# A transformer layer's forward and backward pass on one core: the FFN of chunk 0 placed inside the last attention chunk, and the gradient stage's inputs placed in the memory of FFN weights split into parts

## The chip, the cores and the metric

The kernel runs on one core of a Trainium2 chip. The metric is the device time of one execution in microseconds (us); the smaller the better. A core has TensorE (PE) for matrix products, VectorE (DVE) and ScalarE (ACT) for elementwise work, GpSimd (POOL), which here mostly issues DMAs, and SyncE (SP), which only issues DMAs. Every engine runs its own instructions in order, and they wait for each other by semaphores.

## The reference

One layer with sliding-window attention and an FFN, and the gradients of all its inputs for a given `grad_out`. S is 2048 tokens, D is 512, F is 1792, with 32 heads of 16; everything is bf16.

```python
def attention(x, wqkv, wo):
    q, k, v = split(x @ wqkv)                 # 32 heads of 16
    idx = pos[:, None] - 2 * arange(8)        # 8 keys, every second token back
    logits = einsum("hsd,hswd->hsw", q, k[idx]) * 16 ** -0.5     # masked where idx < 0
    o = einsum("hsw,hswd->hsd", softmax(logits), v[idx])
    return merge_heads(o) @ wo

h  = x + attention(layernorm(x), wqkv, wo)
h2 = h + gelu(layernorm(h) @ w1 + b1) @ w2 + b2
out_0 = h2
out_1 .. out_7 = gradients of (x, wqkv, wo, w1, b1, w2, b2) for grad_out
```

## The kernel before, in words

Tokens are cut into NC = 4 chunks of CH = 512 (four tiles of P = 128 partitions, so DC = 4 tiles of D and FT = 14 tiles of F). There are three stages, each with its pools of SBUF memory. A pool that is released gives its bytes to the next one on the same side, and the first writer of a new tile there then waits for the last readers and writers of the old one.

**Attention** (functions `p1_*`). For each chunk: layer norm (`p1_ln`, DVE with bn_stats), the projections to q, k, v, dots over the eight taps, softmax (`p1_sm1`, `p1_sm2`), then for the output rows `R` gathered from memory by POOL's indirect DMA, eight products `prb` on DVE (L289) reduced by `ps_band` on PE (L294), the permutation back, `wo`, and `h` with the second layer norm, whose result is stored (`ln_d`) and transposed to `ln2T` (L189, L190). `p1_tm` makes the stored forms of q, k and v through the staging tile `tmst` (stores at L242 and L246). The output of a chunk is done in two halves, `p1_o(c, 0)` and `p1_o(c, 1)`, and `p1_d(c)` is its end (the transposition to `ln2T`). The pools `early` (right side: wqkv, xt, tmst and so on) and `late` (left side) serve this stage; `wff` holds `w1` and `w2`, loaded by POOL in two DMAs during chunk 0.

**FFN, forward and backward in one pass over the chunks.** `p2_h(c)` is a generator: for each of four blocks of F (4, 4, 4 and 2 tiles) it makes `ps_h` on PE (L548), bias and square on ACT (L550, L551), and the gelu with its derivative on DVE, nine operations a block (L555 to L564), around one tanh on ACT. The results `gt` and `dt_` are kept, and `gt` is transposed by a DMA on SP into `tst` and stored to `gT_d` by POOL (`tok_store`, L529 to L533). `p2_rest(c)` loads `goT` (grad_out transposed by DMA), makes the output `ps_f2` (L582) and `h2s`, then `ps_gg` = w2T by goT (L595), multiplied with dt on DVE (L598) and stored as `ghT_d`, then `ps_gl2` with w1T (L607) and the layer norm's backward. The loop over chunks runs `p2_h(c + 1)` a block at a time between groups of `p2_rest(c)`. The transposed weights `w1T` and `w2T` are made by two transposing DMAs on SP (L509, L511), and w2T is halved by one DVE operation (L510). `woT` and `wqT` are transposed at the start of chunk 2, `wkT` and `wvT` at the start of chunk 3; all four lie in buffers that were `ln2T` of the chunks (`lnt`), so that they wait for these chunks' `ps_h` to be done. `glf` is the row buffer of dots gradients, with a memset of its end at L504.

In these two stages the order of instructions on each engine is chosen by a scheduler from the order of the text, the dependencies and estimated durations; the order of the text is only its priority.

**Gradients** (from L690). The order is written out by hand. DVE's band products of the backward (`prb`, L906, 96 of 1.2 us) lead, and `slot()` fills PE with the weight gradients of the generator `wgrads`: `ps_gw2` (L789), `ps_gw1` (L798), `ps_gwo` (L808), `ps_gwq` (L818). Their inputs come through two rotating buffers in the pool `gwp`: `r8` (three of 1 MB; gout_r, ln2_r, o_r, ln1_r in halves) and `gwm` (two of 1 MB; pieces of `gT_d`, `ghT_d`), and their results leave through `gwst` (two). `p3` holds the rest: `cf`, `sh`, `ghT`, `got`, `ln1r`, `rows` and others.

Of the kernel before, what the change touches and what calls it, by code (L numbers as in the profile page):

```python
# [36 lines left out]
def kernel(  # L37
# [232 lines left out]
    def coefs(wp, src, off, hs):  # L270
        cf = wp.tile([P, 2, 2, 8, H], BF16, name="cf", tag="cf", bufs=2)
        if hs == 512:
            V.transpose(out=cf[:].rearrange("p a b c h -> p (a b c h)"), in_=_sub(src, [[256, 4], [1, 8], [8, 32]], off))
        else:
            for hf in range(2):
                V.transpose(out=cf[:, hf].rearrange("p b c h -> p (b c h)"),
                            in_=_sub(src, [[256, 2], [1, 8], [8, 32]], off + hf * hs))
        return cf
# [42 lines left out]
    w1 = wff.tile([P, DC, F], BF16, name="w1")  # L321
    w2 = wff.tile([P, FT, D], BF16, name="w2")
# [12 lines left out]
    def p1_ln(c):  # L335
        xt = early.tile([P, TPC, D], BF16, name="xt", tag="xt", bufs=4)
        load_rows(xt, xf, c)
        if c == 0:
            for i in range(3):
                o = (1, 0, 2)[i] * D  # L340
                SY.dma_start(out=wqkv[:, :, o:o + D], in_=A_wqkv[:, o:o + D].rearrange("(a p) j -> p a j", p=P))
        ln1 = early.tile([P, TPC, D], BF16, name="ln1", tag="ln1", bufs=1)
        layernorm(early, xt, rstd1, c, ln1)
        store_rows(ln1_d, c, ln1)
        ln1T = early.tile([P, DC, CH], BF16, name="ln1T", tag="ln1T", bufs=2)
        to_fm(ln1, ln1T)
        st_[c].update(xt=xt, ln1T=ln1T)
# [120 lines left out]
    G.dma_start(out=w1[:], in_=B_w1.rearrange("(a p) f -> p a f", p=P))  # L468
    G.dma_start(out=w2[:], in_=B_w2.rearrange("(a p) d -> p a d", p=P))
    p1_tm(0)  # L470
    for c in range(NC):
        if c + 2 < NC:
            p1_ln(c + 2)
        if c + 1 < NC:
            p1_dots(c + 1)
        if c > 0:
            p1_d(c - 1)
        if c + 2 < NC:
            p1_qk(c + 2)
        if c + 1 < NC:  # L480
            p1_sm1(c + 1)
        p1_o(c, 0)
        if c + 1 < NC:
            p1_v(c + 1)
            p1_sm2(c + 1)
        p1_o(c, 1)
        if c + 1 < NC:
            p1_tm(c + 1)
        if c == 1:
            V.tensor_scalar(out=w2[:], in0=w2[:], scalar1=0.5, scalar2=None, op0=ALU.mult)  # L490
    p1_d(NC - 1)

    pb = TT("pb1")
    T.transpose(pb[:, 0:FT], b1b[:], ident[0:FT, 0:FT])
    V.tensor_copy(out=b1c[:], in_=pb[:, 0:FT])
# [5 lines left out]
    late.release()  # L501
    glp = LP("glp", "right")
    glf = glp.tile([P, 2, SP], BF16, name="glf")
    V.memset(glf[:, :, S:SP], 0.0)  # L504
    ff = LP("ff", "right")
    wfb = LP("wfb")
    w1T = wfb.tile([P, FT, D], BF16, name="w1T")
    w2T = wfb.tile([P, DC, F], BF16, name="w2T")
    SY.dma_start_transpose(out=w2T[:], in_=B_w2)  # L509
    V.tensor_scalar(out=w2T[:], in0=w2T[:], scalar1=0.5, scalar2=None, op0=ALU.mult)  # L510
    SY.dma_start_transpose(out=w1T[:], in_=B_w1)  # L511
# [3 lines left out]
    def load_wT(name, src):  # L515
# [3 lines left out]
    FFT = dict(goT=([P, DC, CH], 1), tst=([P, 16, P], 3), gout=([P, TPC, D], 1), ln2r=([P, TPC, D], 1), dt_=([P, 4, 512], 5),  # L519
               h2s=([P, D], 2), gyr=([P, D], 2), junk=([P, D], 1), u=([P, D], 2), gt=([P, 4, 512], 5),  # L520
               xb=([P, 4, PAD + CH], 2), xa=([P, 2, 4, 512], 2))

    def ft(tag, name=None):
        shp, nb = FFT[tag]
        return ff.tile(shp, BF16, name=name or tag, tag=tag, bufs=nb)
# [9 lines left out]
    def p2_h(c):  # L535
        d = ps2[c]
        d["g"], d["d"] = [], []
        for (f0, f1) in FB:
# [4 lines left out]
            for fp in range(f0, f1, 2):  # L543
                ps = X("ps_h")
                for i in range(2):
                    f = fp + i
                    for dc in range(DC):
                        T.matmul(ps[:, i, :], lhsT=w1[:, dc, f * P:(f + 1) * P], rhs=ln2T[c][:, dc, :],  # L548
                                 start=(dc == 0), stop=(dc == DC - 1))
                    A.activation(out=xb[:, f - f0, :], in_=ps[:, i, :], func=ACT.Identity, bias=b1c[:, f:f + 1])  # L550
                    A.activation(out=x2[:, f - f0, :], in_=ps[:, i, :], func=ACT.Square, bias=b1c[:, f:f + 1])  # L551
            gt = ft("gt")
            dt_ = ft("dt_")
# [16 lines left out]
    def p2_rest(c):  # L570
# [8 lines left out]
        for j in range(TPC):  # L579
            ps = Y("ps_f2")  # L580
            for f in range(FT):
                T.matmul(ps[:], lhsT=gts[f // 4][:, f % 4, j * P:(j + 1) * P], rhs=w2[:, f, :], start=(f == 0), stop=False)  # L582
            T.matmul(ps[:], lhsT=ones_row[:], rhs=b2row[:], start=False, stop=False)
            T.matmul(ps[:], lhsT=ident[:], rhs=h_all[c][:, j, :], start=False, stop=True)
            h2s = ff.tile([P, D], BF16, name="h2s", tag="h2s", bufs=2)
            A.copy(out=h2s[:], in_=ps[:])
            G.dma_start(out=h2f[c * CH + j * P:c * CH + (j + 1) * P, :], in_=h2s[:])
            yield
        for bi, (f0, f1) in enumerate(FB):
            for fp in range(f0, f1, 2):  # L590
                ps = X("ps_gg")
                for i in range(2):
                    f = fp + i
                    for dc in range(DC):
                        T.matmul(ps[:, i, :], lhsT=w2T[:, dc, f * P:(f + 1) * P], rhs=goT[:, dc, :],  # L595
                                 start=(dc == 0), stop=(dc == DC - 1))
# [7 lines left out]
        for j in range(TPC):  # L604
            ps = Y("ps_gl2")
            for f in range(FT):
                T.matmul(ps[:], lhsT=dts[f // 4][:, f % 4, j * P:(j + 1) * P], rhs=w1T[:, f, :],  # L607
                         start=(f == 0), stop=(f == FT - 1))
            t = c * TPC + j
            ln_bwd(ff, ps[:], ln2[:, j, :], rstd2[:, t:t + 1], gout[:, j, :], gh[:, j, :])  # L610
            yield
# [25 lines left out]
    def p3_pre():  # L637
# [7 lines left out]
        to_tm_store(ff, got, 0, go_d, 0, False, stage=lambda: ft("tst", "tmst0")[:, 0:8, :].rearrange("p (a b) f -> p a (b f)", a=2))  # L645
# [19 lines left out]
    run(p2_h(0))  # L665
    for c in range(NC):
# [8 lines left out]
        for k in (4, 4, 3):  # L675
            run(hn, 1)
            run(r_, k)
        run(hn, 1)
        if c == NC - 1:
            pre = p3_pre()  # L680
            for _ in range(TPC):
# [8 lines left out]
    ff.release()  # L690
    wfb.release()
    wff.release()
# [4 lines left out]
    gwp = LP("gwp", "right")  # L697
    wqkvT = [wT[n] for n in ("wqT", "wkT", "wvT")]
    P3T = dict(rows=([P, 10, 512], 3), vw=([P, 4, PAD + CH], 1), ghT=([P, DC, CH], 1), got=([P, 4, CH], 1), gqkvT=([P, 12, CH], 1),
               tmst=([P, 2, 512], 2), prod=([P, W, 512], 3), ln1r=([P, TPC, D], 1), pp=([P, 2, 512], 1), sh=([P, 2, 512], 2),  # L700
               cf=([P, 2, 2, 8, H], 2), gqs=([P, 2, 512], 2), gks=([P, 2, 512], 2), gyr=([P, D], 2))

    def pt3(tag, name=None):
        shp, nb = P3T[tag]
# [12 lines left out]
    def wg_out(pss, dst, r0, c0, width=D, sca=1.0):  # L717
        st = gwp.tile([P, 2, D], BF16, name="gwst", tag="gwst", bufs=2)
# [5 lines left out]
    def load_half(name, src, i):  # L724
        r = gwp.tile([P, HN, D], BF16, name=name, tag="r8", bufs=3)
        SY.dma_start(out=r[:], in_=src[i * HN * P:(i + 1) * HN * P, :].rearrange("(t p) d -> p t d", p=P))
        return r

    def load_perm(name, src, i):
        r = gwp.tile([P, HN, D], BF16, name=name, tag="r8", bufs=3)  # L730
# [7 lines left out]
    def load_t(src, q):  # L738
        t_ = gwp.tile([P, 2, NT, P], BF16, name="gwm", tag="gwm", bufs=2)
        SY.dma_start(out=t_[:].rearrange("p a t f -> p (a t f)"),  # L740
                     in_=src[:, 2 * q:2 * q + 2].rearrange("p a c n -> p (a c n)"))
        return t_

    def load_g3(sel, i):
        if sel == 2:
            t_ = pt3("rows", "gqh")[:, 0:HN, :]
        else:
            t_ = gwp.tile([P, HN, D], BF16, name="gqh", tag="gwm", bufs=2)
# [22 lines left out]
    gout_r = [load_half("gout_r", gof, 0)]  # L771
    tiles = [load_t(gT_d, 0)]
    gout_r.append(load_half("gout_r", gof, 1))
    tiles.append(load_t(gT_d, 1))

    def wgrads():
        ln2_r = [load_half("ln2_r", ln2_d, 0)]
        o_r = []
        for q in range(7):
            if q == 6:  # L780
# [4 lines left out]
                st = gwp.tile([P, 2, D], BF16, name="gwst", tag="gwst", bufs=2)  # L785
# [4 lines left out]
                mid=(lambda: ln2_r.append(load_half("ln2_r", ln2_d, 1))) if q == 6 else None)  # L790
# [3 lines left out]
        o_r.append(load_half("o_r", o_d, 0))  # L794
        for q in range(7):
            g_ = tiles[7 + q]
            for d2 in range(2):
# [3 lines left out]
                    mid=(lambda: o_r.append(load_half("o_r", o_d, 1))) if q == 6 and d2 == 1 else None)  # L801
# [4 lines left out]
        ln1_r = [load_perm("ln1_r", ln1_d, 0)]  # L806
        for k2 in range(2):
# [3 lines left out]
                mid=(lambda: ln1_r.append(load_perm("ln1_r", ln1_d, 1))) if k2 == 1 else None)  # L811
# [115 lines left out]
    def p3_go(c, at=(1, 2, 3, 4)):  # L927
# [13 lines left out]
        def t():  # L941
            to_tm_store(p3, got, 0, go_d, c, False, 2)
# [45 lines left out]
    for c in range(NC + 2):  # L988
# [20 lines left out]
        if c > 0:  # L1009
# [4 lines left out]
            cfv = coefs(p3, st3[c - 1]["sh"][:, 0, 0:1], 0, 512)  # L1014
# [23 lines left out]
        if c < NC:  # L1038
            cfq = coefs(p3, glf[:, 0, 0:1], c * CH, SP)
# [16 lines left out]
        if c > 0:  # L1056
            cfk = coefs(p3, shk[:, 0, 0:1], 0, 512)
# [26 lines left out]
    gwp.release()  # L1084
# [36 lines left out]
```

## Time and profile before

| | us |
|---|---|
| median of 14 runs | 764.92 |
| lowest and highest of them | 756.45, 771.39 |
| the profiled execution, its time | 754.44 |
| the profiled execution, span of the trace | 752.7 |
| PE busy | 625.1 (83%) |
| DVE busy | 531.9 (71%) |
| ACT busy | 369.5 (49%) |
| mean granted TensorE clock | 0.966 |

All times of single instructions in this document come from the one profiled execution and count from its span's start. A row of a timeline gives start, duration, engine with line, operation, tiles, the number of instructions joined in the row, and in brackets the idle time of the engine before it with what released it. A row of a windows table gives the window's limits and length, busy time and number of instructions of each engine, then the granted TensorE clock (1.00 is full), the share of DMA engines that were busy, and GB/s moved. PEclk on the page is the granted clock in 40 slices, in tenths.

### The profile page before, as it was taken

The numbers are of one execution on the slowest core, as the hardware profiler recorded it, in microseconds if no ns is written. First come the engines' busy times: TensorE is split into PE (matmuls) and PEld (weight loads), VectorE is DVE, ScalarE is ACT, GpSimd is POOL, SyncE is SP. The second block draws the span as 40 slices with busy tenths as digits, with TensorE's granted clock in tenths as the row PEclk, the third lists the DMA queues.
The fourth block names the chain that finished last, engine by engine and source line by source line (L and its number), as shares of the span: only waits on it lengthen the run. The fifth ranks groups of instructions, "written<-read, shape, count | busy, mean of one in ns | idle before, by whom it ended". The sixth has DMA issues, their size and how long they took to land. (4 is left out here: it accounts for less than half of the span.)

```text
span 752.7 us, 10189 instructions
## 1 busy us (share of the span) xinstructions
PE 625.1 (83%) x3887; PEld 290.4 (39%) x3948; DVE 531.9 (71%) x774; ACT 369.5 (49%) x561; POOL 153.9 (20%) x195
## 2 busy tenths in 40 slices
PE   3787788576777888888899879979967899898997
PEld 1343343222223333333333433434335566543443
DVE  7779869664986777686695598987857688569400
ACT  2476676547553464455351253583347336554411
POOL 4122434330021021012011114140221014112100
PEclk9999999876899999999999999999989999999999
DMA  8572637758955494395488899976695567898351
GB/s 291 202 269 80 232 108 260 248 133 157 223 107 140 91 265 110 99 261 152 112 169 216 214 326 363 413 267 239 208 403 188 209 220 272 323 290 236 143 160 43
DMA packets 145967, 158.88 MB, mean 211 GB/s; under 512 B 94349, under 2 KB 130238, under 8 KB 139262
## 3 DMA queue, kind: packets, MB, share of 16 engines
q1 hardware_dynamic: 122142, 72.73, 36.7%
q0 software_dynamic: 15888, 79.72, 30.2%
q10 hardware_dynamic: 7888, 5.77, 2.4%
q8 instruction: 31, 0.51, 0.3%
q14 instruction: 18, 0.15, 0.1%
HBM read 87.63 MB, written 48.03 MB: 180 GB/s over the span
## 5 line engine op out<-in xcount | busy, mean ns | idle before, releaser
L906 DVE TENSOR_TENSOR prb<-R,cf 128x2048 bf16<-128x2048 bf16 x96 | 111.3, 1217 | 20.7 <-PE ps_band L914 15.9
L548 PE MATMUL ps_h<-ln2T,w 128*128 128x512 bf16 x222 | 63.0, 410 | 22.8 <-ACT xa L551 18.6
L798 PE MATMUL ps_gw<-gwm,ln_r 128*128 128x256 bf16 x448 | 55.6, 276 | 15.8 <-ACT gwst L721 9.4
L595 PE MATMUL ps_gg<-goT,w2T 128*128 128x512 bf16 x218 | 53.8, 378 | 11.4 <-DVE gb1p L598 8.6
L550 ACT ACTIVATE xb<-ps_h,b1c 128x512 bf16<-128x512 f32 x56 | 38.2, 686 | 43.7 <-PE ps_h L548 42.6
L582 PE MATMUL ps_f<-w,gt 128*128 128x512 bf16 x217 | 53.6, 385 | 2.6 <-DVE gt L559 2.3
L789 PE MATMUL ps_gw<-gout_r,gwm 128*128 128x512 bf16 x215 | 51.6, 380 | 4.2 <-ACT gwst L721 1.8
L355 PE MATMUL ps_qkv<-ln1T,wqkv 128*128 128x512 bf16 x186 | 48.7, 398 | 7.0 <-ACT kt L357 2.0
L798 PEld LDWEIGHTS <-ln_r 128*128 128x128 bf16 x448 | 42.9, 98 | 29.5 <-issue 16.3
L211 ACT ACTIVATE gyr<-ps_gl,rstd 128x512 bf16<-128x512 f32 x32 | 21.9, 686 | 64.0 <-PE ps_gl L970 32.5
L620 DVE TENSOR_TENSOR pr<-got,vw 128x4096 bf16<-128x4096 bf16 x16 | 36.5, 2291 | 14.3 <-ACT c L213 7.0
L548 PEld LDWEIGHTS <-w 128*128 128x128 bf16 x224 | 22.9, 103 | 57.6 <-issue 39.5
L533 POOL DMA_DIRECT2D gT_d<-tst x16 | 12.3, 772 | 156.4 <-DMA tst<-gt 151.7
L818 PE MATMUL ps_gwq<-gqh,ln_r 128*128 128x512 bf16 x188 | 42.4, 379 | 1.4 <-ACT gwst L721 1.1
L289 DVE TENSOR_TENSOR prb<-R,cf 128x2048 bf16<-128x2048 bf16 x32 | 37.3, 1211 | 7.6 <-PE ps_band L294 4.4
L557 ACT ACTIVATE xa<-xa 128x2048 bf16<-128x2048 bf16 (+1 forms) x16 | 27.2, 1698 | 30.1 <-DVE xa L556 30.1
L259 DVE TENSOR_TENSOR pr<-qt,kt 128x4096 bf16<-128x4096 bf16 x16 | 36.0, 2284 | 5.5 <-ACT qt L357 3.4
L551 ACT ACTIVATE xa<-ps_h,b1c 128x512 bf16<-128x512 f32 x56 | 38.1, 685 | 1.6 <-DVE dt__2676 L564 0.4
L916 ACT ACTIVATE gks<-ps_band 128x512 bf16<-128x512 f32 x32 | 19.0, 598 | 39.4 <-PE ps_band L914 34.4
L914 PE MATMUL ps_band<-prb,S 128*32 128x512 bf16 x384 | 30.6, 388 | 8.6 <-ACT got L617 4.4
L595 PEld LDWEIGHTS <-w2T 128*128 128x128 bf16 x224 | 21.6, 97 | 41.4 <-issue 18.5
L240 ACT COPY tmst<-ptm 128x1024 bf16<-128x1024 bf16 x32 | 31.5, 1017 | 6.9 <-PE ptm L237 4.6
(242 smaller groups left out, 1191.6 us busy)
## 6 DMA issues: line engine op xcount, KB each, us to landing
gwm<-gT_d SPq DMA_DIRECT2D x7, 1024.0 KB
gwm<-ghT_d SPq DMA_DIRECT2D x7, 1024.0 KB
gT_d<-tst POOLq DMA_DIRECT2D x12, 512.0 KB, 3.5
ghT_d<-tst POOLq DMA_DIRECT2D x12, 512.0 KB, 5.4
ln_d<-ln POOLq DMA_DIRECT2D x8, 512.0 KB, 4.7
out_dram<-gwst ACTq DMA_DIRECT2D x15, 256.0 KB
w<-in_B_w_dram POOLq DMA_DIRECT2D x2, 1792.0 KB, 10.3
vw<-vf_d SPq DMA_DIRECT2D x4, 528.0 KB
```

The source lines that it names most:

```text
L289: V.tensor_tensor(out=pr[:, hf].rearrange("p j (d h) -> p j d h", h=H), in0=R[:, o:o + 4, :].rearrange("p j (d h) -> p j d h", h=H), in1=c ...
L355: T.matmul(ps[:, gg, :], lhsT=wqkv[:, dc, sel * D + g * P:sel * D + (g + 1) * P], rhs=st_[c]["ln1T"][:, dc, :], start=(dc == 0), stop=(dc ...
L548: T.matmul(ps[:, i, :], lhsT=w1[:, dc, f * P:(f + 1) * P], rhs=ln2T[c][:, dc, :], start=(dc == 0), stop=(dc == DC - 1))
L550: A.activation(out=xb[:, f - f0, :], in_=ps[:, i, :], func=ACT.Identity, bias=b1c[:, f:f + 1])
L551: A.activation(out=x2[:, f - f0, :], in_=ps[:, i, :], func=ACT.Square, bias=b1c[:, f:f + 1])
L582: T.matmul(ps[:], lhsT=gts[f // 4][:, f % 4, j * P:(j + 1) * P], rhs=w2[:, f, :], start=(f == 0), stop=False)
L595: T.matmul(ps[:, i, :], lhsT=w2T[:, dc, f * P:(f + 1) * P], rhs=goT[:, dc, :], start=(dc == 0), stop=(dc == DC - 1))
L620: V.tensor_tensor(out=pr, in0=got[:, g, :].unsqueeze(1).to_broadcast([P, W, 512]), in1=_sub(vw[:, g, PAD:PAD + 512], [[-DIL, W], [1, 512]] ...
L789: pss = yield from mm_pair("ps_gw2", lambda ps, o, i, t, k: T.matmul(ps[:], lhsT=g_[:, o, i * HN + t, :], rhs=gout_r[i][:, t, :], **k), MM ...
L798: pss = yield from mm_pair("ps_gw1", lambda ps, o, i, t, k: T.matmul(ps[:, 0:256].rearrange("p (a f) -> p a f", a=2), lhsT=ln2_r[i][:, t, ...
L818: pss = yield from mm_pair("ps_gwq", lambda ps, o, i, t, k: T.matmul(ps[:], lhsT=ln1_r[i][:, t, (2 * d2 + o) * P:(2 * d2 + o + 1) * P], rh ...
L906: V.tensor_tensor(out=pr[:, 4 * hf:4 * hf + 4].rearrange("p j (d h) -> p j d h", h=H), in0=R[:, o:o + 4, :].rearrange("p j (d h) -> p j d ...
```

## The change

Four things are done.

1. `w1` and `w2` are held as three parts (tiles 0 to 7, 8 to 11, 12 and 13 of F), `w2T` likewise and `w1T` as four (0 to 7, 8 and 9, 10 and 11, 12 and 13). The two loads become six, the two transposing DMAs seven, and the two DVE operations that halve w2 and w2T become three each. The functions `wcol` and `wrow` pick the part. The numbers of matmuls and of their columns are the same.
2. The last attention round ends after `p1_o(3, 0)`. Then `early` is released, `glp` and a first FFN pool `ffA` (xa, xb, tst, and two of the five slots of gt and dt) take its memory; block 0 of chunk 0's `p2_h` is put ahead of `p1_o(3, 1)` and block 1 ahead of `p1_d(3)`. Then `late` is released, the second FFN pool `ffB` (the rest) and `wfb` follow, with the seven transposes. The chunk 3 input tile `xt` lies in `late` in place of `early`. The transposition of the bias b1 into `b1c` moves to the end of round 0. The memset of `glf` is written behind the generator's end.
3. The FFN pools are no longer all released ahead of the gradient stage: `wff` and `wfb` stay to the end, and tiles of the gradient stage take the parts' places by name: the `r8` halves 0 and 1 in `w10` and `w20`, `gwm` in `w2T0` and `w1T0`, `gwst` in `w1T10` and `w1T12`, `cf` in `w2T12` and `w1T8`, `sh` in `w112` and `w212`, and `ghT`, `got`, `ln1r` in `w18`, `w28`, `w2T8`. The pool `gwp` is gone. The numbers of buffers are as before.
4. The two loads of gout_r and the first `gwm` are issued on ACT's DMA queue during the last FFN chunk (before: on SP at the start of the gradient stage).

```diff
-    w1 = wff.tile([P, DC, F], BF16, name="w1")
-    w2 = wff.tile([P, FT, D], BF16, name="w2")
+    W3 = [(0, 8), (8, 12), (12, 14)]
+    W4 = [(0, 8), (8, 10), (10, 12), (12, 14)]
+    def wparts(pl, name, parts, byrow):
+        return [(a, b, pl.tile([P, b - a, D] if byrow else [P, DC, (b - a) * P], BF16, name=f"{name}{a}", tag=f"{name}{a}", bufs=1))
+                for (a, b) in parts]
+    w1 = wparts(wff, "w1", W3, False)
+    w2 = wparts(wff, "w2", W3, True)
...
-        xt = early.tile([P, TPC, D], BF16, name="xt", tag="xt", bufs=4)
+        xt = (early if c < NC - 1 else late).tile([P, TPC, D], BF16, name="xt", tag="xt", bufs=NC - 1 if c < NC - 1 else 1)
...
-    G.dma_start(out=w1[:], in_=B_w1.rearrange("(a p) f -> p a f", p=P))
-    G.dma_start(out=w2[:], in_=B_w2.rearrange("(a p) d -> p a d", p=P))
+    for a_, b_, t_ in w1:
+        G.dma_start(out=t_[:], in_=B_w1[:, a_ * P:b_ * P].rearrange("(a p) f -> p a f", p=P))
+    for a_, b_, t_ in w2:
+        G.dma_start(out=t_[:], in_=B_w2[a_ * P:b_ * P, :].rearrange("(a p) d -> p a d", p=P))
...
         p1_o(c, 0)
+        if c == NC - 1:
+            return
...
-    p1_d(NC - 1)
-    pb = TT("pb1")
-    T.transpose(pb[:, 0:FT], b1b[:], ident[0:FT, 0:FT])
-    V.tensor_copy(out=b1c[:], in_=pb[:, 0:FT])
+        if c == 0:
+            pb = TT("pb1")
+            T.transpose(pb[:, 0:FT], b1b[:], ident[0:FT, 0:FT])
+            V.tensor_copy(out=b1c[:], in_=pb[:, 0:FT])
...
     early.release()
-    late.release()
     glp = LP("glp", "right")
     glf = glp.tile([P, 2, SP], BF16, name="glf")
-    V.memset(glf[:, :, S:SP], 0.0)
-    ff = LP("ff", "right")
-    wfb = LP("wfb")
-    w1T = wfb.tile([P, FT, D], BF16, name="w1T")
-    w2T = wfb.tile([P, DC, F], BF16, name="w2T")
-    SY.dma_start_transpose(out=w2T[:], in_=B_w2)
-    V.tensor_scalar(out=w2T[:], in0=w2T[:], scalar1=0.5, scalar2=None, op0=ALU.mult)
-    SY.dma_start_transpose(out=w1T[:], in_=B_w1)
+    ffA = LP("ffA", "right")
...
+    def block_tiles():
+        k = nblk[0] % NS
+        nblk[0] += 1
+        pl = ffA if k < SA else ffp["B"]
+        return [pl.tile([P, 4, 512], BF16, name=f"{n}{k}", tag=f"{n}{k}", bufs=1) for n in ("gt", "dt")]
...
-    run(p2_h(0))
+    hn = p2_h(0)
+    run(hn, 1)
+    p1_o(NC - 1, 1)
+    run(hn, 1)
+    p1_d(NC - 1)
+    late.release()
+    ffp["B"] = LP("ffB", "right")
+    wfb = LP("wfb")
+    w2T = wparts(wfb, "w2T", W3, False)
+    w1T = wparts(wfb, "w1T", W4, True)
+    for a_, b_, t_ in w2T:
+        SY.dma_start_transpose(out=t_[:], in_=B_w2[a_ * P:b_ * P, :])
+    for _, _, t_ in w2T:
+        V.tensor_scalar(out=t_[:], in0=t_[:], scalar1=0.5, scalar2=None, op0=ALU.mult)
+    for a_, b_, t_ in w1T:
+        SY.dma_start_transpose(out=t_[:], in_=B_w1[:, a_ * P:b_ * P])
+    run(hn)
+    V.memset(glf[:, :, S:SP], 0.0)
...
+    def mtile(name, shp):
+        k = ngm[0] % 2
+        ngm[0] += 1
+        return wfb.tile(shp, BF16, name=name, tag=("w2T0", "w1T0")[k], bufs=1)
...
         for k in (4, 4, 3):
             run(hn, 1)
             run(r_, k)
+            if c == NC - 1 and k == 4 and not gout_r:
+                gout_r += [load_half("gout_r", gof, i, i, A) for i in range(2)]
         run(hn, 1)
         if c == NC - 1:
+            tiles = [load_t(gT_d, 0, A)]
...
-    gwp = LP("gwp", "right")
...
+    HOME = dict(ghT=([P, DC, CH], (wff, "w18")), got=([P, 4, CH], (wff, "w28")), ln1r=([P, TPC, D], (wfb, "w2T8")),
+                sh=([P, 2, 512], (wff, "w112"), (wff, "w212")), cf=([P, 2, 2, 8, H], (wfb, "w2T12"), (wfb, "w1T8")),
+                gwst=([P, 2, D], (wfb, "w1T10"), (wfb, "w1T12")))
...
-    gout_r = [load_half("gout_r", gof, 0)]
-    tiles = [load_t(gT_d, 0)]
-    gout_r.append(load_half("gout_r", gof, 1))
     tiles.append(load_t(gT_d, 1))
```

## The prediction, made before the changed kernel ran

> **What bounds the kernel now.** I read the page's engine rows first, then sums over windows, then the timelines of DVE, PE and SP where the windows show no engine full.
>
> ```profile
> PE 625.1 (83%) x3887; PEld 290.4 (39%) x3948; DVE 531.9 (71%) x774; ACT 369.5 (49%) x561; POOL 153.9 (20%) x195
> PEclk9999999876899999999999999999989999999999
> 140.00:173.00 33.00, 18.84 (x111) 8.05 (x111) 19.29 (x38) 12.93 (x20) 9.30 (x14) 0.75 0.73 202
> 173.00:200.00 27.00, 19.08 (x58) 7.16 (x60) 19.53 (x21) 19.81 (x29) 0.76 (x1) 0.74 0.92 193
> 200.00:229.00 29.00, 21.67 (x87) 8.23 (x87) 21.51 (x27) 17.55 (x25) 4.82 (x7) 0.94 0.62 127
> 161.30:184.80 23.50, 15.25 (x63) 6.61 (x65) 10.19 (x21) 15.31 (x22) 3.94 (x6) 0.75 0.99 191
> 710.00:752.00 42.00, 38.30 (x174) 17.02 (x176) 3.89 (x12) 8.18 (x16) 1.62 (x3) 1.00 0.30 98
> ```
>
> PE leads, but it is not one bound. The 89 us from the last chunk's bands to the first ps_gg have PE at 60 of 89 and DVE at 60, with the granted clock (third figure from the end of a row) at 0.75 in the first 60: the boundary of attention and FFN, where engines wait for each other. The last 42 us are PE at 38.3 with DVE nearly idle: the weight gradients that are left over. So the gradient stage is bound by PE, and idle PE removed anywhere moves the end.
>
> The boundary, by what ended each wait (DVE, then PE, then SP):
>
> ```profile
> 148.26 2.36 DVE L289 TENSOR_TENSOR prb<-R,cf 128x2048 bf16<-128x2048 bf16 x2 [3.09 <-DMA R<-v_d,rowi]
> 166.57 0.07 DVE L504 MEMSET glf<- 128x16 uint32 x1
> 172.92 0.17 DVE L495 CAST b1c<-pb 128x14 f32<-128x14 bf16 x1 [2.07 <-PE pb L494]
> 179.83 0.69 DVE L555 TENSOR_SCALAR xa<-xa 128x2048 bf16<-128x2048 bf16 x1 [6.74 <-ACT xa L551]
> 216.00 0.69 DVE L555 TENSOR_SCALAR xa<-xa 128x2048 bf16<-128x2048 bf16 x1 [1.64 <-ACT xa L551]
> 149.54 0.62 PE L294 MATMUL ps_band<-prb,S 128*32 128x512 bf16 x4 [6.13 <-DVE prb L289]
> 228.72 1.53 PE L595 MATMUL ps_gg<-goT,w2T 128*128 128x512 bf16 x5 [0.20 <-ACT xa L551]
> 141.65 0.36 SPq L242 DMA_DIRECT2D q_d<-tmst  x1
> 161.34 8.41 SPq L509 DMA_TRANSPOSE w2T<-in_B_w_dram  x1
> 169.89 10.28 SPq L511 DMA_TRANSPOSE w1T<-in_B_w_dram  x1
> 186.47 1.92 SPq L532 DMA_TRANSPOSE tst<-gt  x1
> 188.84 2.09 SPq L574 DMA_TRANSPOSE goT<-in_grad_out_dram  x1
> 201.37 3.10 SPq L517 DMA_TRANSPOSE woT<-in_A_wo_dram  x1
> 451.86 0.82 PE L789 MATMUL ps_gw<-gout_r,gwm 128*128 128x512 bf16 x3 [1.54 <-DMA gwm<-gT_d]
> ```
>
> Between the last band and the first gelu, DVE waits 3.69 (before 162.49), 1.37, 1.14, 2.07 and 6.74: 15 us with nothing to do, while chunk 0's gelu could run, had it been released. Its first gelu operation is at 179.83, its last ends at 214.36. SP's row is free from 142 to 161.
>
> **The change part by part.**
>
> *Begin the FFN early.* In the changed order 40 of the 56 ps_h matmuls of chunk 0 come ahead of the end of chunk 3's wo, some inside the 6.13 gap; blocks 0 and 1 of the gelu stand between and behind the eight prb. But the scheduler also puts the memset of glf directly ahead of the first prb. It takes memory of the staging tile tmst, and so waits for the q_d stores. The one of 141.65 is slow: the DMA row of 139 to 153 moves bytes until about 152.3, its completion comes at 152.58. Before, the memset ran at 166.57 and waited for nothing. All bands are queued behind it on DVE, and PE's ps_band behind those: they start at 152.58, not 148.26, **+4.3**.
>
> From there DVE is full: eight prb and the row op 9.3, ln 1.3, two gelu blocks 16.2 (four TENSOR_SCALAR at 0.62 and five TENSOR_TENSOR at 1.1 make 8.1), four bn pairs at 0.78 = 3.1, first ops 0.6: 30.5, so block 1 ends at 183.1. xa has two buffers, so the last ps_h needs that, one activation (0.7) and four matmuls (0.9): T = 184.9 or so. Of chunk 0's 35 us of gelu (179.83 to 214.36) half is then done.
>
> *SP's queue.* Here stands the new wait. The order on SP is now: q_d, two tst, then woT's transpose, then w2T in three parts, w1T in four, two tst, goT. woT takes the memory of ln2T0, so it waits for the last ps_h of chunk 0, at T; everything listed after it, which before ran from 161.34, waits with it. From T: woT 3.1, w2T 8.41, w1T 10.28, gaps 0.7, two tst 2.5 and 1.3: 26.3, so goT is issued at 211.2. In before it landed 4.3 after its issue (193.14), so ps_gg begins at 215.5 instead of 228.72: **−13.2**. PE by itself (f2 of chunk 0 and 28 ps_h of chunk 1) would be there at about 205, so some 10 us of new PE wait take the place of the removed ones.
>
> Transposes in parts were not seen before. Lower bound: the same bytes, 0. Middle: two tst sizes, 512 KB 1.92 and 256 KB 1.26, leave 0.6 fixed for an issue; five more make 3.0. Upper: a slice of columns is dearer than a whole matrix (wvT 5.08 against woT 3.10 for 512 KB), +6 for w1T's parts. The rows of the same kind are nearest to the middle; I take +1.5 in all, since part of the 10.28 was contention with gT_d and ln_d stores (ln_d took 10.6 us to land there): boundary −11.7, between −7 and −20.
>
> [...] Row: 161.3 to 184.8 moved the 3.67 MB of w2T and w1T at DMA share 0.99 and 191 GB/s. [...] Row: 0.75 clock; after the 6.13 wait the clock records stay at half from 146.0 to 156.2. [...]
>
> *w2T scaling, three operations in place of one.* On DVE before dt2, waiting for w2T0, which lands near 197: chunk 1's gelu then begins near 202 instead of 216, ahead of PE. Cost 0; the cover is SP's wait. If SP gets later, dt2 is later with it.
>
> *w1 and w2 in six loads; xt elsewhere; b1c moved.* POOL idles 2.52, 6.46 and 8.17 between 14 and 34 us, more than four more issues (0.8 each by its gT_d row) need. b1c's 0.16 and 0.17 go to round 0. 0, between −1 and +2.
>
> *Gradient inputs early.* The two gout_r and the first gwm go from SP after the stage starts (439.43, 445.76, 445.26) to ACT's queue in the last FFN chunk. They wait there for w10's, w20's and w2T0's last readers, all past; three more issues on ACT at 49% are nothing. Removed: PE's 1.54 at 451.86. In 440 to 452 PE has 8.0 of 12 with the DMA share at 1.00, DVE 11.97: DVE's bands hold that stretch, the filler fills it. I take −1.0, between 0 and −4. Buffer counts (r8 three, gwm two) are as before, so the rotation is not faster and the 6 us wait for ln_r near 550 stays: 0.
>
> Sum: −11.7 −1.0 = −12.7 on the profiled execution (752.7 span, 754.44 its time): 741.7. It lies 1.4% under the median of 14 runs, 764.92; in the same ratio 752.0. I say **753**.
>
> **The rivals.**
>
> [...]
>
> *B. Nothing.* The transposes' parts and goT eat what the gelu saves: chain 35 to 44 us, ps_gg at 220 to 229: 758 to 766. For it: every part waits behind woT. Against: chunk 1's gelu work has been pulled ahead and is not lost.
>
> *C. Slower: head of line on SP.* Of the seven transposes behind woT, the two of 1 MB cost twice wvT's 5.08 and the five smaller ones 5.08 each: 45.9 instead of 18.7, so ps_gg is at 242.7, +14, the end near **779**. It decides from the point where the chain from T exceeds 44 us (31 by my sum), or T slips past 198. For it: wqT, wkT and wvT, slices like w1T's parts, cost 4.20 to 5.08. Against: w2T's parts are whole rows, and two thirds of the bytes are in parts as large as a whole weight.
>
> *D. It does not do what it says.* DVE or PE order could keep the gelu behind the bands; the order shows it interleaved, so I give this no share of its own beyond B.
>
> **How the numbers follow.** Main case, boundary −7 to −20 (746 to 758): 0.58. A (736 to 746): 0.14. B (758 to 768): 0.13. C (above 768): 0.12, and 0.03 for collisions in the gradient stage that end there too. Half a per cent, 3.8 us, is about what a measurement of this kernel can tell from no change, so the band is 761.1 to 768.7. Faster: the main case, A, and the better part of B that ends under 761: 0.75; same 0.10; slower 0.15. The range for 8 in 10 runs from 738 (leaving out half of A's best) to 771. The main case's own range is 746 to 758.
>
> **What would show it.** Right: first prb near 152.6 after the glf memset, DVE nearly without waits until block 1 ends near 183; SP's woT near 185 and seven weight transposes summing to 19 to 22; ps_gg first at 214 to 219, with PE waiting about 10 for goT or w2T ahead of it; no gwm wait near the first ps_gw2. Wrong: first ps_gg after 225 with the transposes summing over 30 (C); first ps_gg near 205 (A); prb at 148; or PE idle in the gradient stage above the page's by more than 4 us, by gwst, sh or cf waiting in their new homes.

## The result and the profile after

The changed kernel takes 745.59 us (median of 10 runs) against 765.03 (47 runs of before): ratio 0.9832, 95% interval 0.9792 to 0.9872, 12.9 us of 765. Applied to the 764.92 that the prediction stood on, that is 752.1; predicted were 753. Two more series of runs gave 0.9806 (0.9760 to 0.9853) and 0.9805 (0.9768 to 0.9843). The profiled execution is 745.67, its span 743.8. One experiment, two_orders, has a profile of a disturbed execution, of which only distances inside the boundary are used.

First the page's engine row and clock row after, then windows:

```profile
PE 621.2 (84%) x3885; PEld 288.2 (39%) x3948; DVE 529.9 (71%) x778; ACT 368.8 (50%) x561; POOL 155.0 (21%) x199
PEclk9999999988899999999999999999989999999999
140.00:173.00 33.00, 20.92 (x119) 8.09 (x122) 23.22 (x32) 22.11 (x32) 8.90 (x11) 0.90 0.40 124
173.00:200.00 27.00, 19.04 (x79) 7.55 (x80) 22.87 (x39) 15.22 (x22) 5.18 (x6) 0.81 0.85 193
200.00:213.30 13.30, 10.11 (x44) 3.92 (x44) 9.59 (x11) 9.82 (x15) 2.75 (x4) 1.00 1.20 224
```

The busy times of the whole span are as before; the work has moved closer together. From 140 to 173 us, ACT goes from 12.93 to 22.11 and DVE from 19.29 to 23.22, and the boundary of attention and FFN is over at 213.3 instead of 228.7. The timelines at the same places (DVE, PE, SP, and PE again at the start of the gradient stage):

```profile
147.31 0.18 DVE L197 BATCH_NORM_AGGREGATE mv<-st 128x2 f32<-128x6 f32 x1 [6.82 <-DMA q_d<-tmst]
147.32 0.07 DVE L708 MEMSET glf<- 128x16 uint32 x1
147.61 2.36 DVE L289 TENSOR_TENSOR prb<-R,cf 128x2048 bf16<-128x2048 bf16 x2
153.52 0.69 DVE L581 TENSOR_SCALAR xa<-xa 128x2048 bf16<-128x2048 bf16 x1
201.97 0.69 DVE L581 TENSOR_SCALAR xa<-xa 128x2048 bf16<-128x2048 bf16 x1 [1.07 <-ACT xa L578]
181.68 1.44 PE L575 MATMUL ps_h<-ln2T,w 128*128 128x512 bf16 x3 [2.66 <-ACT xa L578]
194.88 0.60 PE L608 MATMUL ps_f<-w,gt 128*128 128x512 bf16 x2 [1.72 <-DVE gt L585]
208.59 2.18 PE L575 MATMUL ps_h<-ln2T,w 128*128 128x512 bf16 x8 [0.49 <-ACT xa L578]
213.29 2.84 PE L621 MATMUL ps_gg<-goT,w2T 128*128 128x512 bf16 x11 [2.52 <-DMA goT<-in_grad_out_dram]
137.74 0.53 SPq L242 DMA_DIRECT2D q_d<-tmst  x1
183.57 2.06 SPq L531 DMA_TRANSPOSE woT<-in_A_wo_dram  x1
186.14 9.04 SPq L702 DMA_TRANSPOSE w2T<-in_B_w_dram  x3
195.22 8.73 SPq L706 DMA_TRANSPOSE w1T<-in_B_w_dram  x4
204.06 4.87 SPq L559 DMA_TRANSPOSE tst<-gt  x2
209.04 1.86 SPq L600 DMA_TRANSPOSE goT<-in_grad_out_dram  x1
433.91 1.24 PE L852 MATMUL ps_gw<-gout_r,gwm 128*128 128x512 bf16 x3
```

The chain has the predicted links in the predicted order. The glf memset stands directly ahead of the first prb, and the 6.82 us of waiting for the q_d store, shown in the row just before it, end as it starts. The gelu (153.52) runs among the bands. woT is issued on SP when the last ps_h of chunk 0 (181.68) is done, the seven weight transposes follow, then goT, and ps_gg waits for goT. That wait is 2.52 us, not ten. Chunk 1's gelu starts at 201.97. In the last row the first ps_gw2 no longer waits for gwm.

The absolute times shift with what happened earlier in each profile, so from here the boundary is measured from the issue of the last q_d store to the first ps_gg. The prediction's sum turns into 75.4 on that scale (87.07 less 11.7). Stages in the table run from start to start of the instructions named.

| profile | q_d to prb | q_d to ps_gg | PE idle before ps_gg | FFN, first ps_gg to last ps_gl2 | last ps_gl2 to first ps_gw2 | first ps_gw2 to end |
|---|---|---|---|---|---|---|
| before | 6.61 | 87.07 | 0.20 | 211.4 | 11.7 | 300.8 |
| after | 9.88 | 75.55 | 2.52 | 208.3 | 12.3 | 309.9 |
| again | 11.57 | 77.06 | 2.38 | 211.1 | 11.1 | 303.7 |
| third | 11.22 | 77.45 | 2.91 | 211.7 | 12.3 | 302.8 |
| early_ffn_alone | 11.57 | 77.51 | 2.99 | 210.5 | 10.4 | 303.7 |
| takeover_alone | 11.48 | 92.96 | 0.20 | 211.4 | 10.9 | 308.5 |
| bias_alone | 6.77 | 87.09 | 0.20 | 214.3 | 12.0 | 309.8 |
| wot_later | 10.60 | 73.17 | 0.20 | 211.5 | 11.1 | 308.1 |
| glf_behind | 5.78 | 71.74 | 3.32 | 210.0 | 12.4 | 306.6 |
| weights_whole | 10.59 | 74.34 | 0.91 | 212.6 | 10.4 | 305.4 |
| all_three | 6.52 | 68.99 | 0.20 | 217.4 | 10.4 | 301.4 |
| two_orders | 5.56 | 68.83 | 0.20 | | | |
| all_h2s4 | 6.65 | 69.44 | 0.20 | 213.4 | 10.4 | 302.6 |
| take_h2s4 | 5.69 | 66.99 | 0.20 | 211.3 | 12.6 | 301.4 |

### The profile page after: what moved, and what is told of

Its sections match the earlier page's. It is cut to its first block, busy times and chain, and to the rows that moved or that the text cites. A ratio compares the mean times of both kernels' runs of the same rounds, so it can differ in the third digit from the quotient of the medians.

```text
span 743.8 us, 10203 instructions
## 1 busy us (share of the span) xinstructions
PE 621.2 (84%) x3885; PEld 288.2 (39%) x3948; DVE 529.9 (71%) x778; ACT 368.8 (50%) x561; POOL 155.0 (21%) x199
## 5 line engine op out<-in xcount | busy, mean ns | idle before, releaser
L969 DVE TENSOR_TENSOR prb<-R,cf 128x2048 bf16<-128x2048 bf16 x96 | 111.5, 1220 | 25.4 <-PE ps_band L977 20.3
L575 PE MATMUL ps_h<-ln2T,w 128*128 128x512 bf16 x219 | 60.6, 394 | 16.2 <-ACT xa L578 12.4
L624 DVE CUSTOM_DVE_ANT_0 dt<-ps_gg,dt 128x512 bf16<-128x512 f32 x56 | 38.0, 689 | 37.5 <-PE ps_gg L621 37.5
L633 PE MATMUL ps_gl<-w1T,dt 128*128 128x512 bf16 x218 | 55.6, 387 | 2.8 <-DVE gb1p L624 1.7
L852 PE MATMUL ps_gw<-gout_r,gwm 128*128 128x512 bf16 x215 | 53.2, 389 | 2.8 <-ACT gwst L798 1.8
L372 PE MATMUL ps_qkv<-ln1T,wqkv 128*128 128x512 bf16 x185 | 47.1, 390 | 6.7 <-ACT kt L374 2.1
L881 PE MATMUL ps_gwq<-gqh,ln_r 128*128 128x512 bf16 x188 | 44.1, 390 | 2.0 <-DMA ln_r<-ln_d 1.8
L977 PE MATMUL ps_band<-prb,S 128*32 128x512 bf16 x384 | 31.3, 394 | 11.3 <-DVE prb L969 6.3
L560 POOL DMA_DIRECT2D gT_d<-tst x16 | 12.4, 775 | 124.8 <-DMA tst<-gt 124.8
```

What stands on the lines that cost most here:

```text
L372: T.matmul(ps[:, gg, :], lhsT=wqkv[:, dc, sel * D + g * P:sel * D + (g + 1) * P], rhs=st_[c]["ln1T"][:, dc, :], start=(dc == 0), stop=(dc ...
L575: T.matmul(ps[:, i, :], lhsT=wcol(w1, dc, f), rhs=ln2T[c][:, dc, :], start=(dc == 0), stop=(dc == DC - 1))
L624: V.tensor_tensor_reduce(out=dsl, in0=ps[:, i, :], in1=dsl, scale=1.0, scalar=0.0, op0=ALU.mult, op1=ALU.add, accum_out=gb1p[:, f, c:c + 1])
L852: pss = yield from mm_pair("ps_gw2", lambda ps, o, i, t, k: T.matmul(ps[:], lhsT=g_[:, o, i * HN + t, :], rhs=gout_r[i][:, t, :], **k), MM ...
L881: pss = yield from mm_pair("ps_gwq", lambda ps, o, i, t, k: T.matmul(ps[:], lhsT=ln1_r[i][:, t, (2 * d2 + o) * P:(2 * d2 + o + 1) * P], rh ...
L969: V.tensor_tensor(out=pr[:, 4 * hf:4 * hf + 4].rearrange("p j (d h) -> p j d h", h=H), in0=R[:, o:o + 4, :].rearrange("p j (d h) -> p j d ...
```

## The experiments

There are three series, and the kernels of a series share its runs of before: again to bias_alone, wot_later to all_three, third to take_h2s4. Ratios are to before, with their 95% intervals. The changed kernel itself did not run in the second series, so comparisons of those ratios with its own go across series.

### Which half of the change carries it, and is the loss in the gradient stage real?

The first pair of profiles has a puzzle: 15.4 us earlier at ps_gg, 8.9 at the end. The gradient stage took 309.9 against 300.8. The theory was that the boundary makes the gain; the rival, that the early gradient inputs make part of it, and that the stage's loss belongs to the change.

**again**: no edit.

> The changed kernel as it is, once more. In its first profile the gradient stage (first ps_gw2 matmul to the end of the span) took 309.9 us against 300.8 before, and five spells of half clock lay in it against two. If the change itself brings these spells, they stand at the same matmuls again and the stage takes 308 to 311 again. [...] Ratio to before 0.978 to 0.988 either way; first ps_gg near 213.

Measured 0.9806 (0.9760 to 0.9853). The same program's gradient stage took 303.7, and 302.8 in the third profile. In the first of these three, half-clock spells (granted clock 0.50 in the middle of each) lay at 434, 478, 543, 560 and 683; in the second at 436, 484, 545 and 559; in the third at 438, 544 and 558. Most recur and some do not, and the stage took less than the 308 to 311 expected if the change brings them, so that it brings them is not shown. The spells don't explain the times either: the mean granted clock from the first ps_gw2 to the end is 0.97 in the first two profiles, which differ by 6.2 us, and 0.98 in the third. And bias_alone, whose gradient stage is that of before, took 309.8. So 301 to 310 is the scatter of single profiles, and the nine us that the first pair seemed to give back can't be put down to the change. The averages, 305.9 for seven profiles with the changed stage (two_orders left out) and 304.0 for the six with the old one, leave room for some two us.

**early_ffn_alone**: the first two stages as changed, the gradient stage as before.

```diff
     ffA.release()
+    wfb.release()
+    wff.release()
...
     p3 = LP("p3")
+    gwp = LP("gwp", "right")
...
-                gout_r += [load_half("gout_r", gof, i, i, A) for i in range(2)]
...
-            tiles = [load_t(gT_d, 0, A)]
...
+    gout_r = [load_half("gout_r", gof, 0)]
+    tiles = [load_t(gT_d, 0)]
```

> Only the early FFN: parts, order and pools of the first two stages as changed, the gradient stage with the pools, buffers and SP loads of before. Theory 1 (the gain is the boundary's): ratio 0.978 to 0.988 like the changed kernel, first ps_gg near 213, the gwm wait of about 1.5 us back, the 2.9 us wait of the first ps_band of the gradient stage gone. Theory 2 (the early gradient inputs are worth a good part): 0.988 to 0.995.

Measured 0.9761 (0.9701 to 0.9820): the whole gain, and by its centre some more than the 0.978 set as its lower end. ps_gg is at 77.51 as in the changed kernel; the gwm wait is back, at 1.04 us.

**takeover_alone**: everything as changed, but chunk 0's FFN and the bias transposition stand behind the attention again.

```diff
-    hn = p2_h(0)
-    run(hn, 1)
-    p1_o(NC - 1, 1)
-    run(hn, 1)
-    p1_d(NC - 1)
-    late.release()
+    hn = p2_h(0)
```

with `p1_o(NC - 1, 1)`, `p1_d(NC - 1)`, b1c, the releases and the glf memset ahead of it in the order of before.

> Only the memory: parts, homes, pools and early gradient loads as changed, but the FFN of chunk 0 and the bias transposition stand behind the attention again. Theory 1: ratio 0.997 to 1.006, first ps_gg at 226 to 233 (the glf memset still stands ahead of the bands and costs up to 4). Theory 2: ratio 0.985 to 0.995.

Measured 0.9993 (0.9957 to 1.0028), ps_gg at 231.13: no gain in sum. With the memset ahead of the bands, prb comes 11.48 us behind the store (6.61 in before) and ps_gg 92.96 (87.07), so the boundary is 5.9 us longer, 0.8% of the whole. The ratio does not show this loss; where it comes back is not known, so this run does not say what the takeover alone is worth.

```profile
149.36 0.18 DVE L197 BATCH_NORM_AGGREGATE mv<-st 128x2 f32<-128x6 f32 x1 [8.08 <-DMA q_d<-tmst]
149.36 0.07 DVE L527 MEMSET glf<- 128x16 uint32 x1
182.11 0.69 DVE L584 TENSOR_SCALAR xa<-xa 128x2048 bf16<-128x2048 bf16 x1 [6.74 <-ACT xa L581]
```

The first two rows of this DVE timeline show 8.08 us of waiting for the store of q_d ahead of the memset. The last shows before's 6.74 us wait ahead of the first gelu back in place. So the takeover of memory alone doesn't let the FFN begin sooner.

**bias_alone**: before with one edit, which tests whether b1c was the gate.

```diff
+        if c == 0:
+            pb = TT("pb1")
+            T.transpose(pb[:, 0:FT], b1b[:], ident[0:FT, 0:FT])
+            V.tensor_copy(out=b1c[:], in_=pb[:, 0:FT])
...
-    pb = TT("pb1")
-    T.transpose(pb[:, 0:FT], b1b[:], ident[0:FT, 0:FT])
-    V.tensor_copy(out=b1c[:], in_=pb[:, 0:FT])
```

> The kernel before with one edit: b1c is made at the end of round 0. In before the first xb of the FFN waits for b1c (172.92), and the order here puts ps_h and its activations earlier. If b1c was the gate, the first gelu operation comes right behind ln at about 171 in place of 179.83 and the ratio is 0.988 to 0.993 (5 to 9 us of the boundary). If DVE's bands and ln2T set the pace anyway, 0.997 to 1.003.

Measured 0.9987 (0.9953 to 1.0021): it was not. The first gelu operation is at 175.37, 30.5 behind the first prb (31.6 in before). ACT's first xb still stands behind its ln2T copies of chunk 3:

```profile
167.20 1.93 ACT L190 COPY ln2T<-pt 128x1024 bf16<-128x1024 bf16 x2 [4.68 <-PE pt L189]
169.15 0.69 ACT L551 ACTIVATE xb<-ps_h,b1c 128x512 bf16<-128x512 f32 x1
175.37 0.69 DVE L556 TENSOR_SCALAR xa<-xa 128x2048 bf16<-128x2048 bf16 x1 [8.98 <-ACT xa L552]
```

In the changed kernel, where chunk 0's blocks stand in the attention's text, ACT has its first xb at 139.79 and the first of those copies at 156.14. No other way of moving xb ahead was tried.

### The waits that the prediction named

**wot_later**: an order edge on SP, no wait.

```diff
-            load_wT("woT", A_wo)
+            with tc.issue_after(ffp["go0"].ins):
+                load_wT("woT", A_wo)
```

> The changed kernel, with woT's transpose issued behind goT of chunk 0 on SP (an order edge, no wait), so that nothing ahead of w2T waits for the last ps_h of chunk 0. w2T should be issued near 177 in place of 186, goT near 200 in place of 209. If the head-of-line wait on SP set the first ps_gg (as predicted: PE idle before it), it moves with goT, to 204 to 207, ratio near 0.972. If PE's own work ends at 210.8 as the trace after shows (only 2.5 us of idle ahead of ps_gg), it moves by 2.5 at most and the ratio stays within 0.3% of the changed kernel's.

SP and PE in its timelines:

```profile
177.75 9.37 SPq L702 DMA_TRANSPOSE w2T<-in_B_w_dram  x3
187.18 10.02 SPq L706 DMA_TRANSPOSE w1T<-in_B_w_dram  x4
201.96 2.33 SPq L600 DMA_TRANSPOSE goT<-in_grad_out_dram  x1
211.60 1.75 PE L621 MATMUL ps_gg<-goT,w2T 128*128 128x512 bf16 x6 [0.20 <-ACT xa L578]
```

The head-of-line wait, an instruction that could start but stands in a queue behind one that waits, is real: without it w2T is issued at 177.75, and goT 63.5 behind the q_d store instead of 71.3 to 73.2. But ps_gg moves only to 73.17, and no longer waits for goT (0.20): PE's own work ends there. That is the second reading. The ratio, 0.9681 (0.9651 to 0.9711), fell by more than these 2.4 to 4.3 us say and missed what both readings expected; the profile doesn't show the rest, and it is left open.

**glf_behind**:

```diff
-    V.memset(glf[:, :, S:SP], 0.0)
+    tc.keep_in_program_order(V.memset(glf[:, :, S:SP], 0.0))
```

> The changed kernel, with the memset of glf kept behind chunk 0's last gelu operation on DVE. In the runs with the early memset the first prb of the last chunk comes 10 to 11.5 us behind the issue of the last q_d store, in those without 6.6 to 6.8. Prediction's step: prb at 6.7 behind the store, ps_gg 3 to 5 us earlier, ratio 0.3 to 0.6% below the changed kernel's. Rival: the DVE chain waits elsewhere later (for xa or ps_h) and gives it back: ps_gg within 1 us of before.

DVE, SP and PE in its timelines:

```profile
144.39 2.36 DVE L289 TENSOR_TENSOR prb<-R,cf 128x2048 bf16<-128x2048 bf16 x2 [2.64 <-DMA R<-v_d,rowi]
205.90 2.32 SPq L600 DMA_TRANSPOSE goT<-in_grad_out_dram  x1
210.35 2.02 PE L621 MATMUL ps_gg<-goT,w2T 128*128 128x512 bf16 x6 [3.32 <-DMA goT<-in_grad_out_dram]
```

The first row now waits for the gather R, as in before, 5.78 behind the store. The gain reaches ps_gg (71.74, 3.8 to 5.7 earlier), since the last ps_h of chunk 0 and with it SP's chain come earlier. Measured 0.9722 (0.9678 to 0.9766), 0.9% under the changed kernel's 0.9806 and 0.9805 of the other series, more than the 0.3 to 0.6% expected. The step was right in its us, and the rival falls.

**weights_whole**: early_ffn_alone with `W3 = W4 = [(0, 14)]`.

> Only the early FFN, with w1, w2, w1T and w2T in one piece each (two transposing DMAs instead of seven), the gradient stage as before. Prediction's step put +1.5 on the seven parts (0 to 9). If parts cost, the two transposes here sum to 14 to 16.5 us and ps_gg comes 1.5 to 3 us earlier than in the early FFN alone with parts; if not, they sum to 17 to 18.5 and nothing moves (ratio within 0.3% of 0.976).

```profile
187.44 8.97 SPq L701 DMA_TRANSPOSE w2T<-in_B_w_dram  x1
196.46 7.22 SPq L705 DMA_TRANSPOSE w1T<-in_B_w_dram  x1
```

In one piece they take 16.2 us, in parts 17.5 (durations alone, in early_ffn_alone and in after; 18.0 in third): by these single profiles the parts cost 1.3 to 1.8 us. ps_gg comes 3.2 us earlier, 1 of them because prb does. Measured 0.9747 (0.9708 to 0.9786), not to be told from early_ffn_alone's.

**all_three**: early_ffn_alone with the memset behind the gelu and a different order on SP.

```diff
+    ffp["goT0"] = ft("goT")
+    ffp["go0"] = SY.dma_start_transpose(out=ffp["goT0"][:], in_=gof[0:CH, :])
+    with tc.issue_after(ffp["go0"].ins):
+        for a_, b_, t_ in w1T:
...
+            with tc.issue_after(ffp["w1l"].ins):
+                load_wT("woT", A_wo)
```

> The early FFN in parts with the gradient stage of before, the glf memset behind the gelu, goT of chunk 0 ahead of w1T, and woT behind w1T. If the gains add: the last q_d store to first ps_gg falls from 75.5 to about 68 to 71 us and the ratio is 0.967 to 0.973. If PE's own work ends the boundary: about 72 us, ratio 0.971 to 0.976.

ps_gg is at 68.99, as it is if the gains add, and the ratio is 0.9614 (0.9582 to 0.9645), a larger gain than expected. But the FFN stage took 217.4 us. ACT and then POOL in its timelines near 264:

```profile
264.72 0.59 ACT L613 CAST h2s<-ps_f 128x512 bf16<-128x512 f32 x1 [6.91 <-DMA out_dram<-h2s]
257.15 0.71 POOL L560 DMA_DIRECT2D gT_d<-tst  x1 [5.65 <-DMA tst<-gt]
258.67 1.10 POOL L614 DMA_DIRECT2D out_dram<-h2s  x2
```

ACT waits 6.91 us for an h2s buffer (there are two), whose store is queued on POOL behind a gT_d store that waits for its transpose. PE idles 3.61 behind it.

### What is left when they are taken away

**third**: the changed kernel, for the comparison in this series.

> The changed kernel a third time, as the measure for the other kernels of this series. Ratio 0.978 to 0.985; the first ps_gg 75.5 to 77.5 behind the last q_d store, as in its two profiles so far.

0.9805 (0.9768 to 0.9843), as expected.

**two_orders**: the changed kernel with the edits of wot_later and glf_behind.

> The changed kernel with both order edges: woT behind goT of chunk 0 on SP, and the glf memset behind the gelu on DVE. Alone they brought the first ps_gg from 75.5 to 77 behind the last q_d store to 73.2 and 71.7. If they add, 68 to 70, and the ratio lies 0.8 to 1.1% under the changed kernel's. If the PE work is the bound once SP is not, 70 to 72, and 0.5 to 0.8%.

ps_gg is at 68.83: they add. The ratio, 0.9590 (0.9536 to 0.9644), lies further below third's than expected, by 2.2%. It rests on few executions; the medians of all of them, 739.34 against 748.47, say 1.2%.

**all_h2s4**: all_three with `h2s=([P, D], 4)`.

> The kernel all_three with h2s in four buffers in place of two. There ACT waited 6.9 us near 264 for a store of h2s, queued on POOL behind a gT_d store that waits for its transpose, and PE idled 3.6 behind it: the FFN stage took 217.4 us against 208 to 212 elsewhere. If that wait is the cause, the FFN stage is at 210 to 214, and the ratio 0.3 to 0.8% under 0.9614. If the stage was long for another reason, 216 to 218, and no change.

No h2s row in its list of waits names a store any more, and the FFN stage took 213.4, inside the expected range. The ratio, 0.9623 (0.9582 to 0.9663), does not tell it from all_three; the 0.3 to 0.8% expected were not seen.

**take_h2s4**: all_h2s4 with the changed kernel's gradient stage.

> The kernel all_h2s4 with the gradient stage of the changed kernel (takeover of the parts' memory, early loads on ACT) in place of the one before. If the takeover is worth the 1 us of the prediction, its ratio is 0.1 to 0.3% lower than all_h2s4's; if its R gather (which waits for the FFN's tile u there) costs what the early gwm brings, within 0.2%; if it costs more, 0.2 to 0.5% higher.

Measured 0.9651 (0.9605 to 0.9697), by its centre 0.3% above all_h2s4, with overlapping intervals. The kernels all_three, all_h2s4 and two_orders are the fastest of this study, some 2% below the changed kernel's ratio of the same or another series; among themselves they can't be ordered.

## Why the prediction was right, step by step

**Early FFN, right in mechanism and size.** Predicted ps_gg 11.7 earlier. From the q_d store it is 75.55 to 77.45 in three profiles against 87.07 and 87.09 (before and bias_alone): 9.6 to 11.5, mean 10.4. early_ffn_alone gives the whole gain, weights_whole gives it without the parts, bias_alone shows none from b1c, and takeover_alone has the late gelu back: so the early FFN carries it. That the sum of 75.4 fits so closely is in part luck: two of its terms are off and cancel, as shown below. Block 1 ends at 180.84 by its dt (179.63 and 1.21); with prb at 147.61 that is 33.2 us, against 30.5 predicted; two waits for ACT, 1.97 and 0.89 us, are most of the difference.

**The memset, right.** +4.3 predicted; prb comes 3.3 to 5.0 later behind the q_d store with it. glf_behind has these us back, and 4 to 6 at ps_gg; there the operation that showed the 6.82 us wait runs at 141.37 without it. The text put it behind the FFN's generator; the scheduler's order decided.

**SP's queue, right in what waits for what; its terms were off.** Counted from the q_d store (141.65 in the prediction's rows, 137.74 after), woT was put at 43.3 and was issued at 45.8, and at 47.4 and 47.3 in again and third. From woT to goT the sum had 27.8 with the parts, and it took 25.4 to 26.0. From goT to ps_gg it had 4.3, and it took 4.2. So woT came 2.6 to 4.1 us late, and SP's chain took 1.8 to 2.4 us less.

The step that failed in size is "PE by itself would be there at about 205", 63.4 on this scale. PE's own work ended at 210.77, which is 73.0, nearly ten us later than that, so the new wait is 2.5 us and not 10. PE's f2 of chunk 0 itself waited for the gelu (1.72 us at 194.88 for gt), and the last ps_h ahead of ps_gg stood behind f2 (208.59). So ps_gg near 205, with f2 as the bound (A, to which the prediction gave 0.14), was not to be had by faster transposes: wot_later brought goT 8 to 10 us forward and ps_gg 2.4 to 4.3, and the shortest boundary of all profiles, in take_h2s4, is 66.99.

**Transposes in parts.** +1.5 was taken between 0 and 9; weights_whole shows 1.3 to 1.8. Rival C needed 45.9 us for the seven (by its own figures 45.7), and they took 17.5. For the 3.67 MB of both weights 17.5 us are 210 GB/s, and 16.2 us in two pieces are 227, near the 196 of before's 18.69 us. Other stores ran beside them in both kernels (an ln_d store landed in 4.9 us here, in 10.6 in before), so the rate without them isn't shown. The measured rate of before was the one to use.

**The clock.** The prediction's sum has no term for it, and none was needed: PE waited 2.52 us for goT, and the granted clock is 1.00 from 200 to 213.3, and from 213.3 to 225 as well. What a wait of ten us would have cost was not tested.

**Scaling w2T.** Its third part waited 0.38 us for the transpose (198.08) and chunk 1's gelu began at 201.97. The prediction had 202, which on the scale of the q_d store is 60.4 against 64.2, so it came 3.9 us later.

**w1 and w2 in six loads, xt, b1c: 0.** No cost is seen: the last q_d store is issued at 136.4 to 138.6 in the changed kernel and its variants, and at 138.10 in bias_alone, which has the old loads; the 141.65 of before's profile is the odd one. b1c's move alone is worth nothing.

**Gradient inputs early: −1.0 predicted, wrong.** The gwm wait went: from the first prb of the stage to the first ps_gw2 it takes 2.7 to 3.0 us with the takeover, 3.8 to 5.4 without. But the stretch from the last ps_gl2 to the first ps_gw2 did not get shorter: 11.9 us on average in after, again and third, against 11.7 in before. With the early FFN it takes 12.0 on average of six profiles with the takeover, and 10.4 in each of the four without; in the order of before, 10.9 with it (takeover_alone) and 11.7 and 12.0 without. The step that failed is the one that counts the buffers ("r8 three, gwm two"), finds them as before and puts their new places at nothing: the counts are as before, the places aren't. POOL's first gather of the stage, in after, in early_ffn_alone and in take_h2s4:

```profile
420.32 1.48 POOL L251 DMA_INDIRECT R<-k_d,rowi  x1 [5.08 <-DVE u L222]
419.20 2.06 POOL L251 DMA_INDIRECT R<-k_d,rowi  x1 [0.31 <-issue]
412.48 2.30 POOL L251 DMA_INDIRECT R<-k_d,rowi  x1 [4.00 <-PE ps_gl L634]
```

In after it starts 1.3 us ahead of the last ps_gl2; in early_ffn_alone it goes at once, 7.4 us ahead, and the first prb is 3.0 us sooner behind that ps_gl2. What it waits for is most likely dt, which ps_gl2 reads, and not u. The view names u in after, but other tiles of DVE in again, third and wot_later, and ps_gl in take_h2s4. Common to all is the PE: the gather starts 0.67 us after the start of the eighth of the last 14 ps_gl2 matmuls in six profiles with the takeover and two h2s buffers, and 0.67 us after the fourth in take_h2s4, whose four h2s buffers shift the memory. The eighth is the last reader of block 1's dt, the fourth that of block 0's. Another place for R's buffer was not tried.

**The sum.** −12.7 predicted, −12.9 to −14.9 in the three measurements of the changed kernel. The prediction's sum had 11.7 in the boundary and 1.0 in the gradient stage; the profiles show the boundary's 10.4 and no gain in the gradient stage. The other 2.5 to 4.5 are not pinned to a stage, and that the total came so close is luck in that part: attention and FFN are each about 2.5 shorter by the averages of these single profiles, less than they scatter. The ratios of again and early_ffn_alone, and of take_h2s4 and all_h2s4, are by their centres 0.3 to 0.5% higher with the takeover than without, with overlapping intervals: a small loss is likelier than the gain of 1.0 us.

## What to carry to other kernels

Moving a later stage's work into an earlier one's waits paid here once the text moved it: an input made ready sooner (b1c) did nothing (0.9987) while its consumers stood behind others in the order of their engine. Then read the new order on every queue for early-ready instructions that take over memory: one memset and one transpose, ahead of work they have nothing to do with, kept back 8 of the 18 us that this boundary gave at most in two_orders (77 and 69 against 87), and an order edge for each gave them back. Buffers that come to lie in other memory can inherit waits that their count doesn't show: here POOL's first gather of R waited 5.08 us in after and 0.31 in early_ffn_alone.

## What the runs showed of the hardware

The same program's gradient stage took 302.8, 303.7 and 309.9 us in three profiles, with half-clock spells (0.50, as at 435 to 437 in after) that partly recur and partly don't, at a mean granted clock of 0.98, 0.97 and 0.97: a difference of 9 us in one pair of profiles said nothing. An instruction that waits for a q_d store beside the gathers of R started only 9.6 to 11.3 us after the store's issue (the memset's start less the store's issue in after, again, early_ffn_alone and takeover_alone). Whether the gathers are the reason was not tested.
